# Cosformer attention into a squared-ReLU layer on one core: features of batch 1's queries and keys apart, and a new order of all operations

## The chip, the core and the metric

The kernel runs on one core of one Trainium2 chip. The core has a matrix engine (TensorE, PE in the profile; its weight loads are PEld), a vector engine (VectorE, DVE), an activation engine (ScalarE, ACT), GpSimd (POOL) and SyncE (SP). Each runs its own instructions in order and waits for the others through semaphores. POOL, SP and ACT also issue DMAs. The metric is the device time of one execution in microseconds (us), the median of several runs; before the change it is 275.71 us (275.62 to 275.82, 3 runs).

## What is computed

Attention with cosine and sine features, without a softmax, and then two matrix products with a squared ReLU between them. There are 8 batches of 576 rows, 8 heads of 64 columns; the second part works on 4608 tokens of 512 columns, with 2048 hidden ones.

```python
def phi(x, c, s):
    r = np.maximum(x, 0.0)
    return np.concatenate([r * c, r * s], axis=-1)
q_p = phi(q, cos_w, sin_w)
k_p = phi(k, cos_w, sin_w)
kv = np.einsum('bhsf,bhsd->bhfd', k_p, v)
z = np.sum(k_p, axis=2)
num = np.einsum('bhsf,bhfd->bhsd', q_p, kv)
den = np.einsum('bhsf,bhf->bhs', q_p, z)[..., None] + 1e-06
x = (num / den)            # then heads side by side: 4608 x 512
h = x @ w_in               # 512 -> 2048
out = np.maximum(h, 0) ** 2 @ w_out
```

## The kernel before

**Batches and stages.** Each batch of 576 rows is cut into four blocks of 128 rows (j = 0 to 3) and a tail of 64 rows (t). For each batch b the kernel loads keys and queries into one float32 tile kq (1 MB each) with their tails in kqt, and the values in three parts into vs and vst (`ldkB`, `ldqB`, `ldktB.g`, `ldqtB.g`, `ldvB.i`). It makes the features in bfloat16: `cosB.j` and `sinB.j` (the functions `cos_part`, `sin_part`, L451 on DVE, L449 on ACT) write the tile fe, their tails the tile fet. `vsB.i` spreads the values into vext (L433). `kvB` multiplies key features with values on PE (40 matmuls, tile kz), `kvzB` copies the result out. The query features are turned on PE (`qTB.j`, copied by `qTcB.j`) for batches 0 and 1 and by a transposing DMA on SP (`qTdB.i`) for the others. `numB.j` is the numerator and denominator on PE, `divB.j` the division on DVE (three instructions, L599 to L605) into xp, and xp is turned again (`xTB.j` and `xTcB.j`, or the DMA `xTdB.i`) into xT.

The second part takes xT. For batch 0 and part of 1 and 2 it is a plain product `HB.s.tokhalf` (four or eight matmuls, tile hps), then its ReLU (`...r`) and square (`...q`). For the rest it is a two-by-two product with seven instead of eight blocks: `GB.s.P1` to `P7` with sums `xsB.n` of xT and `w1sn` of the weights, and with evacuations `seed`, `u2`, `s5`, `c11r`, `c12r`, `c21r`, `c22r`. The last product is `Y0.a0` to `a15` and `b0` to `b15` for batch 0 (tile yh, plain; `a` for the first half of the tokens, `b` for the second), and `YB.P1` to `P7` with sums `YB.Sn` and `w2tn` for the others; `YB.stI` stores.

**What sets the order.** The prologue is written out by hand. All the rest is a set of operations in a planner (class Plan), with an engine, a list of predecessors and the tiles that each uses; the string ORDER gives the sequence in which they are emitted, and with it the order on every engine. A star behind a name puts an operation on ACT that could also go to DVE. The planner's own estimates pick the slots of the tiles. Loads that are issued ahead of the planned part are entered with `plan.given(name, time)`: the time at which the order assumes that they have landed. These are the four quarters each of w_in and w_out (`w1_in`, `w2_in`), the query tail of batch 0 (`qt0`), and q, k, their tails and v of batch 1.

**The queue of early loads.** POOL issues, in order, the first loads of batch 0, the four quarters of w_in, the query tails of batch 0 and the first quarter of w_out. Behind the last of the four query features of batch 0 (`cos0.2`, `cos0.3`, `sin0.2`, `sin0.3`, the list `first`), `loads_of_1` issues on POOL q, its tails, k, its tails, the second quarter of w_out, v of batch 1, and the last two quarters of w_out. Loads of batch 2 are on POOL too, at the places that ORDER gives them: `ldv2.0` stands in it ahead of the last of these features. Loads from batch 3 on are on SP, beside the transposing DMAs and the stores. kq has one slot, so a load of the next batch waits until the features of the last one are made; vs has one slot also.

**Products that wait for early loads.** `H0.s.tokhalf` needs a quarter of w_in each. `Y0.a0` to `a3` and `Y0.b0` to `b3` need the first quarter of w_out and a square of H0, `a4` and `b4` on need the second, `a8` and `b8` the third, `a12` and `b12` the fourth. `qT1.j` needs query features, `kv1` all key features and the spread values.

Of the kernel before, what the change touches and what calls it, by code (L numbers as in the profile page):

```python
# [25 lines left out]
num0.3 div0.3 xT0.2 H0.3.00.0 xT0.3 H0.2.00.0 xTc0.2 xTc0.3* H0.1.10.0 H0.1.10r H0.2.10.0
H0.2.00r* H0.0.01.0 H0.0.01r* H0.1.01.0 H0.1.01r* H0.0.10.0 H0.2.10r* H0.1.11.0 f0.t1 H0.0.00r
H0.1.00r H0.1.00q H0.3.00r Y0.a0 f0.t0* qT0.4 H0.0.10r H0.1.10q H0.0.11.0 H0.0.11r* w1s1 Y0.a1
Y0.a2 H0.2.11.0 qTc0.4* H0.2.11r* w1s2 w1s4 Y0.a3 H0.2.01.0 cos1.3 H0.1.11r* H0.2.01r* H0.3.10.0
H0.3.10r* H0.3.10q sin1.0* Y0.b0 Y0.b1 Y0.b2 Y0.b3 H0.3.01.0 H0.3.00q sin1.3* sin1.t cos1.t  # L30
H0.3.11.0 H0.3.11r cos1.1 Y0.b4 H0.3.01r* Y0.b5 Y0.b6 Y0.a4 Y0.a5 cos1.2* sin1.1* qT1.4 qTc1.4*
vs1.1* sin1.2 qT1.3 ldqt2.1 Y0.a6 Y0.a7 cos1.0 qT1.0 vs1.0 qTc1.3* vs1.2 kv1 H0.3.11q* qT1.1
H0.1.01q Y0.a8 Y0.a9 Y0.b7 qTc1.1 kvz1* num1.1 ldq2 qTc1.0 qT1.2 H0.1.11q* Y0.b8 Y0.b9 Y0.b10
div1.1 xT1.1 qTc1.2* num1.2 ldk2 H0.3.01q* ldkt2.1 w2t1 Y0.b11 Y0.b12 Y0.b13 Y0.b14 div1.2 xT1.2
w2t2 xTc1.1* num1.0 ldqt2.0 div1.0 Y0.b15 xTc1.2* Y0.c10* w2t3 Y0.a10 vs2.0* Y0.a11 Y0.a12
ldkt2.0 xT1.0 xTc1.0* num1.3 div1.3 Y0.a13 ldqt3.0 Y0.a14 Y0.c11* Y0.a15 Y0.c00 ldqt3.1
H1.2.00.0 H1.2.00r ldv2.2 xT1.3 ldv2.1 sin2.1 H1.0.01.0 Y0.c01* Y0.st0 xTc1.3* H1.1.11.0 cos2.1
cos2.0* H1.3.10.0 H1.0.01r* ldkt3.0 H1.1.01.0 H1.3.10r* cos2.2* sin2.0 cos2.3 sin2.2 sin2.3
H1.3.00.0 H1.3.00r* vs2.2* H1.0.00.0 sin2.t* H1.1.11r* H1.2.10.0 cos2.t Y0.st1 vs2.1 ldkt3.1
H1.0.10.0 H1.0.10r qTd2.0 qTd2.1 ldv3.0 w2t4 H1.2.10r* H1.3.10q H1.2.01.0 H1.1.01r* H1.1.01q*  # L40
kv2 kvz2* ldv3.2 H1.1.10.0 H1.1.10r* H1.1.10q* H1.2.01r* ldk3 num2.1 div2.1 H1.1.00.0 H1.1.00r*
H1.0.11.0 H1.3.00q num2.2 H1.2.11.0 H1.3.11.0 H1.0.11r* ldq3 H1.2.11r* H1.0.00r H1.1.00q* div2.2
num2.3 H1.1.11q H1.3.11r* H1.3.01.0 H1.3.01r* H1.3.01q* Y1.P10 div2.3 num2.0 Y1.seed Y1.P11
Y1.seed1 ldqt4.1 H1.3.11q vs3.2 Y1.P20 vs3.0* Y1.P21 Y1.c111* Y1.S1 Y1.S2 Y1.P6 xTd2.1 div2.0
Y1.S3 Y1.c110 Y1.u2* cos3.0* sin3.1 cos3.1 cos3.2* sin3.0 sin3.2 sin3.3* num1.4 div1.4 cos3.3*
Y1.P5 ldv4.2 Y1.S4 ldv3.1 vs3.1 H2.1.10.0 xTd2.0 xs2.1 H2.1.10r* qTd2.2 H2.0.11.0 H2.0.11r*
sin3.t* Y1.P7 qTd3.0 xT1.4 xTc1.4 Y1.s5 Y1.c22 xs2.2 H2.0.00.0 G2.2.P1 qTd3.1 H2.1.00.0 xs2.4
ldv4.0 H2.0.01.0 cos3.t* kv3 H2.1.00r* H2.0.00r* G2.2.seed H2.1.11.0 kvz3* xs2.3 H2.0.01r
H2.1.00q num3.0 div3.0 vs4.2* ldk4 H2.1.11r* H2.1.11q G2.2.P2 G2.2.c11r* ldq4 H2.1.01.0 ldkt4.0
w1s3 G2.2.P6 qTd3.2 num3.1 ldqt4.0 H2.1.01r* H2.1.01q* vs4.0* div3.1 G2.2.u2* H2.0.10.0 H2.0.10r  # L50
Y1.P3 Y1.c12 ldv4.1 num3.2 H2.1.10q* div3.2 ldv5.2 G2.2.P5 G2.3.P1 G2.2.s5* G2.3.seed G2.2.P7
G2.2.c22r G2.3.P5 num3.3 xTd3.0 G2.3.s5* div3.3 xTd3.1 G2.3.P2 G2.3.c11r* G2.3.c11q G2.3.P6
Y1.st0 G2.3.u2* G2.2.P4 G2.2.c21r* sin4.3* G2.2.P3 G2.2.c12r ldkt4.1 cos4.1 G2.3.P3 ldkt5.0
# [30 lines left out]
G5.3.seed G5.2.P6 G5.1.c22q* sin7.3 G5.2.P3 G5.2.u2 G5.2.c12r G5.2.P2 xTd6.0 G5.2.c11r* G5.3.P6
G5.3.P2 G5.2.P7 G5.2.c22r G5.3.c11r qTd6.2 G5.3.u2* vs7.1* G5.3.P5 G5.3.s5* G5.1.c11q G5.3.P7
cos7.3* Y4.P4 Y4.c21* xTd6.1 G6.0.P1 G5.3.c22r G5.3.P4 cos7.t* G5.3.c21r* G6.0.seed sin7.t
G5.3.P3 cos7.2 G5.2.P4 kv7 G5.3.c11q xs6.1 G6.0.P5 xs6.2 G6.0.P6 G6.1.P1 G5.3.c12r qTd7.0
G5.3.c22q xs6.3 G6.0.u2 kvz7* num7.0 div7.0 Y4.st1 G6.0.s5* G5.2.c21r* Y5.P1 G5.1.c21q* Y5.seed
G5.3.c21q G6.0.P3 num7.1 G6.0.c12r G6.0.P2 G6.1.seed qTd7.2 Y4.st0 G5.3.c12q Y5.S1 qTd7.1 Y5.P2
# [1493 lines left out]
```

## Time and profile before

| what | value |
|---|---|
| median of 3 runs | 275.71 us |
| the profiled execution, whole | 275.77 us |
| its span, first to last instruction | 273.5 us |
| mean granted TensorE clock | 0.996 |
| ACT busy | 191.0 us, 70% |
| moved by DMA | 53.0 MB, 194 GB/s over the span |
| PE's last matmul ends | 268.8 us |

The page and the timelines give every instruction of each engine with its start from the span's start, its duration, and in square brackets how long the engine stood idle before it and what ended that time. A group of equal instructions in a row is one line with its count (x8). DMA issues are instructions of the engine that issues them; the time to landing is listed apart. The chain of waits goes back from the last instruction, at each step to what released it. Line numbers are those of the kernel before.

The mean share of the sixteen DMA engines is 0.99 to 1.16 in the stretches up to 160 us (it can pass 1 as packets of several queues overlap) and 0.15 from 200 us on.

### The profile page before, as it was taken

How to read it: one execution, taken by the hardware profiler on the slowest of the kernel's cores; microseconds unless marked ns; L12 is line 12 of the kernel's file. 1: busy time of each engine (PE TensorE's matmuls, PEld its weight loads, DVE VectorE, ACT ScalarE, POOL GpSimd, SP SyncE). 2: the span in 40 equal slices, each digit the busy share in tenths (PEclk: the TensorE clock that was granted, in tenths of full speed). 3: DMA queues.
4: the chain of work that ended last, by engine and by line, in shares of the span. 5: the costliest groups of instructions: out<-in, count | busy, mean ns of one | idle time of the engine just before them, and what ended most of it. 6: DMA issues, size and time to landing. Idle time of an engine off the chain costs nothing.

```text
span 273.5 us, 6782 instructions
## 1 busy us (share of the span) xinstructions
PE 264.0 (97%) x2787; PEld 224.0 (82%) x2792; DVE 223.8 (82%) x399; ACT 191.0 (70%) x298; POOL 29.0 (11%) x47
## 2 busy tenths in 40 slices
PE   8999989999999999999999999999999999999993
PEld 3578657689889888999888998799988888888882
DVE  3775887978998999999899998999847948888941
ACT  5754489699688997898799866984669447656300
POOL 8934536100000000000000000000000000000000
PEclk9999999999999999999999999999999999999998
DMA  6999999799999999999996999757142000110116
GB/s 220 318 205 273 343 292 296 225 296 242 293 164 286 301 248 252 354 209 292 210 362 119 232 264 301 159 175 101 36 116 98 0 2 1 76 80 2 77 35 198
DMA packets 79006, 53.00 MB, mean 194 GB/s; under 512 B 52064, under 2 KB 74592, under 8 KB 78976
## 3 DMA queue, kind: packets, MB, share of 16 engines
q1 hardware_dynamic: 71344, 38.28, 57.4%
q0 software_dynamic: 7040, 13.76, 19.0%
q10 hardware_dynamic: 592, 0.52, 0.6%
q8 instruction: 22, 0.36, 0.5%
q14 instruction: 8, 0.07, 0.1%
HBM read 36.70 MB, written 9.44 MB: 169 GB/s over the span
## 4 chain that ended last, share of the span: by engine, by line
PE 75%; DMA 14%; POOL 4%; DVE 2%; ACT 1%; issue 1%; SPq 0%; DVEq 0%; POOLq 0%; ACTq 0%
PE ya L462 17%; PE yb L462 14%; PE hb L462 12%; PE hc L462 8%; PE ha L462 8%; DMA w1sb<-in_moe_w_in_dram 5%; PE hps L462 4%; PE yh L462 4%; DMA kq<-in_q_dram 3%; DMA kqt<-in_k_dram 3%; PE kz L462 3%; DMA xT<-xp 3%; PE num L462 3%; PE yc L462 2%; POOL kq L503 1%; POOL w1sb L412 1%
## 5 line engine op out<-in xcount | busy, mean ns | idle before, releaser
L462 PEld LDWEIGHTS <-w1sb 128*128 128x128 bf16 x736 | 70.5, 98 | 9.6 <-issue 0.9
L462 PEld LDWEIGHTS <-gs 128*128 128x128 bf16 x512 | 49.5, 98 | 6.6 <-DVE gs L459 0.8
L462 PEld LDWEIGHTS <-gT 128*128 128x128 bf16 x448 | 43.1, 98 | 11.7 <-issue 1.5
L462 PE MATMUL hps<-xT,w1sb 128*128 128x256 bf16 x320 | 38.2, 273 | 0.5 <-DMA xT<-xp 0.4
L443 ACT ACTIVATE gT<-gT 128x1024 bf16<-128x1024 bf16 x35 | 36.7, 1061 | 2.1 <-DVE gT L456 1.7
L449 ACT ACTIVATE fe<-kq,cols 128x1024 bf16<-128x1024 f32 (+1 forms) x34 | 33.7, 1032 | 3.5 <-DMA kq<-in_k_dram 2.9
L462 PEld LDWEIGHTS <-w1s 128*128 128x128 bf16 x312 | 29.8, 98 | 3.8 <-issue 0.4
L451 DVE TENSOR_SCALAR fe<-kq,cols 128x1024 bf16<-128x1024 f32 (+1 forms) x38 | 25.4, 705 | 6.7 <-DMA kq<-in_k_dram 5.6
L462 PE MATMUL ya<-w2sb,gT 128*128 128x256 bf16 x256 | 30.7, 273 | 0.1
L462 PE MATMUL hb<-xs,w1sb 128*128 128x256 bf16 x208 | 30.1, 272 | 0.1
L462 PE MATMUL ha<-xT,w1sb 128*128 128x256 bf16 x176 | 26.2, 272 | 0.0
L445 DVE TENSOR_TENSOR gT<-gT 128x1024 bf16<-128x1024 bf16 x37 | 24.9, 685 | 0.2
L605 DVE TENSOR_TENSOR xp<-num,den 128x512 bf16<-128x512 f32 (+1 forms) x33 | 22.2, 675 | 1.1
L456 DVE CUSTOM_DVE_ANT_0 gT<-hb,s 128x512 bf16<-128x512 f32 x26 | 17.8, 686 | 4.8 <-PE hb L462 4.5
L437 ACT ACTIVATE gT<-hps 128x512 bf16<-128x512 f32 x29 | 16.3, 592 | 7.7 <-PE hps L462 7.0
L433 ACT COPY hb<-ha 128x512 f32<-128x512 f32 x26 | 15.2, 586 | 8.7 <-PE ha L462 3.7
L459 DVE TENSOR_TENSOR gs<-gT 128x2048 bf16<-128x2048 bf16 x16 | 19.5, 1220 | 1.2 <-ACT gT L443 0.9
L456 DVE CUSTOM_DVE_ANT_0 gT<-hc,u 128x512 bf16<-128x512 f32 x26 | 17.7, 685 | 2.6 <-PE hc L462 2.4
L433 ACT COPY u<-hb 128x512 f32<-128x512 f32 x21 | 12.3, 586 | 6.5 <-PE hb L462 6.4
L462 PE MATMUL yh<-w2sb,gT 128*128 128x512 bf16 x60 | 14.9, 379 | 1.7 <-DVE fet L451 1.1
L437 ACT ACTIVATE gT<-hb 128x512 bf16<-128x512 f32 x23 | 13.5, 596 | 4.1 <-PE hb L462 3.2
L462 PE MATMUL hc<-xs,w1s 128*128 128x256 bf16 x104 | 15.6, 272 | 0.3 <-DVE gT L456 0.3
(113 smaller groups left out, 415.1 us busy)
## 6 DMA issues: line engine op xcount, KB each, us to landing
...
```

The lines of the kernel that those rows point to most:

```text
L412: nc.gpsimd.dma_start(out=w1sb[:, :, f0:f1], in_=moe_w_in[:, f0:f1].rearrange("(kb p) f -> p kb f", p=P),)
L433: (nc.scalar.copy if e == "ACT" else nc.vector.tensor_copy)(out=out, in_=in_)
L437: nc.scalar.activation(out=out, in_=in_, func=ACTF.Relu)
L443: nc.scalar.activation(out=out, in_=in_, func=ACTF.Square)
L445: nc.vector.tensor_tensor(out=out, in0=in_, in1=in_, op=ALU.mult)
L449: nc.scalar.activation(out=out, in_=in_, func=ACTF.Relu, scale=col)
L451: nc.vector.tensor_scalar(out=out, in0=in_, scalar1=0.0, scalar2=col, op0=ALU.max, op1=ALU.mult)
L456: nc.vector._custom_dve(dve_ops.TENSOR_ADD_SAT, out=out, in0=in0, in1=in1, s0=BIG, s1=0.0)
L459: nc.vector.tensor_tensor(out=out, in0=in0, in1=in1, op=op)
L462: nc.tensor.matmul(out=out, lhsT=lhsT, rhs=rhs, start=start, stop=stop, skip_group_check=True)
L503: eng.dma_start(out=kq[b][:, "kq".index(nm)][:, hs, js], in_=main_of(nm, b)[:, hs, js])
L605: nc.vector.tensor_tensor(out=x, in0=n4[:, :, :, 0:D].rearrange("p b (k l) d -> p b k l d", l=2), in1=r.rearrange("p b (k l) -> p b k l", l=2)
```

## The change

In `plan_att`, the features of batch 1 become operations for the keys alone (`cos1.jk`, `sin1.jk`, needing k) and for the queries alone (`cos1.jq`, `sin1.jq`, needing q): twenty operations of half the width in place of ten. `kv1` then needs those of the keys, `qT1.j` those of the queries of the same block. The other batches keep their operations. The assumed landing times of the first loads are later. ORDER is another sequence of all operations; the sequence is over a thousand words long, and its first lines are shown. On POOL it moves `ldv2.0` from ahead of `loads_of_1` to behind it (behind `qT1.4` in the sequence), and the small loads of batch 2's tails change places with each other. PE has as many instructions as before (5586 with the weight loads), DVE 378 in place of 367 in the listing that joins equal neighbours.

```diff
 ORDER = """
-xT0.k0 sin0.2* cos0.3 xTc0.k0 xT0.k2 ldv2.0 cos0.2* qT0.2 sin0.3* qTc0.2 xT0.k3 xTc0.k2 qT0.3
-xTc0.k3* H0.1.00.0 num0.2 H0.1.00.1 H0.1.00.2 H0.0.00.0 H0.0.00.1 H0.0.00.2 div0.2 qTc0.3*
...
+xT0.k0 cos0.2* sin0.2* sin0.3 xT0.k2 xTc0.k0 cos0.3* qT0.2 xT0.k3 qT0.3 H0.0.00.0 qTc0.2 num0.2
+div0.2 xTc0.k2* H0.0.00.1 xTc0.k3* H0.0.00.2 H0.1.00.0 H0.1.00.1 H0.1.00.2 qTc0.3* num0.3 xT0.2
...
+H0.0.01.0 H0.0.01r* cos1.2q H0.3.10q* cos1.tq sin1.3q H0.2.11.0 H0.2.11r H0.3.01.0 H0.3.01r*
+qT1.4 ldv2.0 Y0.b3 sin1.2q* qT1.0 qTc1.0* cos1.1q cos1.3k qTc1.4* Y0.a0 Y0.a1 Y0.a2 Y0.a3
+cos1.1k* cos1.tk sin1.0k* cos1.0k* qT1.1 cos1.3q qT1.3 cos1.2k Y0.b4 sin1.tk Y0.a4 Y0.a5 vs1.0*
+sin1.1k* qTc1.1 Y0.b5 Y0.b6 Y0.b7 Y0.a6 sin1.2k qT1.2 vs1.1 sin1.3k* H0.1.11q* vs1.2 kv1 Y0.a7
...
@@ def plan_att(b, got, ve, pe):
-        for j in range(J):
-            n = 2 * H * D
-            c = plan.op(
-                f"cos{b}.{j}",
-                both(0.2 + n * 0.00083, 0.135 + n * 0.00052),
-                lambda e, j=j: cos_part(e, b, j),
-                [got["k"], got["q"]],
-                [kq[b], fe[b, j // 2]],
-            )
...
+        sets = [("", ("k", "q", "kt", "qt"), every[0])]
+        if b == 1:
+            sets = [(nm, (nm, nm + "t"), part) for nm, part in (("k", k_), ("q", q_))]
+        for nm, needs, a in sets:
+            main = [got[x] for x in needs if x in "kq"]
+            tail = [o for x in needs if x not in "kq" for o in got[x]]
+            for j in range(J + 1):
+                n = (a.stop - a.start) * (H if j < J else HH) * D
+                for name, emit in (
+                    ("cos", cos_part if j < J else cos_tail),
+                    ("sin", sin_part if j < J else sin_tail),
+                ):
+                    o = plan.op(
+                        f"{name}{b}.{j if j < J else 't'}{nm}",
+                        both(0.2 + n * 0.00083, 0.135 + n * 0.00052),
+                        lambda e, j=j, a=a, emit=emit: emit(e, b, *((j, a) if j < J else (a,))),
+                        main if j < J else tail,
+                        [kq[b], fe[b, j // 2]] if j < J else [kqt[b], fet[b]],
+                    )
+                    if nm != "q":
+                        f.append(o)
+                    if nm != "k":
+                        fq.setdefault(j // 2, []).append(o)
+                        fq.setdefault((j // 2, j), []).append(o)
...
-        w1_in = [plan.given(f"w1.{i}", t) for i, t in enumerate((16.3, 19.4, 21.9, 24.4))]
-        w2_in = [plan.given(f"w2.{i}", t) for i, t in enumerate((26.5, 35.3, 41.2, 44.4))]
-        qt0 = plan.given("qt0", 24.2, [kqt[0]])
+        w1_in = [plan.given(f"w1.{i}", t) for i, t in enumerate((16.5, 19.5, 22.2, 24.6))]
+        w2_in = [plan.given(f"w2.{i}", t) for i, t in enumerate((27.6, 37.2, 42.4, 45.6))]
+        qt0 = plan.given("qt0", 24.6, [kqt[0]])
...
-            ("q", 29.4, kq[1]), ("k", 32.8, kq[1]),
+            ("q", 30.4, kq[1]), ("k", 33.7, kq[1]),
         )}
-        got["qt"] = [plan.given("qt1", 29.8, [kqt[1]])]
-        got["kt"] = [plan.given("kt1", 33.2, [kqt[1]])]
-        land = [plan.given(f"v1.{i}", t, [vs[1, i]]) for i, t in enumerate((36.7, 38.3, 38.8))]
+        got["qt"] = [plan.given("qt1", 30.9, [kqt[1]])]
+        got["kt"] = [plan.given("kt1", 34.2, [kqt[1]])]
+        land = [plan.given(f"v1.{i}", t, [vs[1, i]]) for i, t in enumerate((38.0, 39.4, 39.8))]
```

More of the change, by code (lines that the diff above doesn't have):

```diff
@@ L23 @@
 ORDER = """
-xT0.k0 sin0.2* cos0.3 xTc0.k0 xT0.k2 ldv2.0 cos0.2* qT0.2 sin0.3* qTc0.2 xT0.k3 xTc0.k2 qT0.3
-xTc0.k3* H0.1.00.0 num0.2 H0.1.00.1 H0.1.00.2 H0.0.00.0 H0.0.00.1 H0.0.00.2 div0.2 qTc0.3*
[L26 to L53, printed above, removed]
@@ L84 @@
[L84 to L89, printed above, removed]
@@ new lines @@
+qTc0.4* H0.1.01.0 H0.1.01r w1s1 H0.1.11.0 H0.1.11r* H0.1.00q* H0.2.00r* H0.3.00q* H0.0.11r* w1s2
+Y0.b0 Y0.b1 Y0.b2 sin1.1q H0.3.10.0 H0.3.10r sin1.0q* sin1.tq H0.3.11.0 H0.3.11r cos1.0q
+H0.0.01.0 H0.0.01r* cos1.2q H0.3.10q* cos1.tq sin1.3q H0.2.11.0 H0.2.11r H0.3.01.0 H0.3.01r*
+qT1.4 ldv2.0 Y0.b3 sin1.2q* qT1.0 qTc1.0* cos1.1q cos1.3k qTc1.4* Y0.a0 Y0.a1 Y0.a2 Y0.a3
+cos1.1k* cos1.tk sin1.0k* cos1.0k* qT1.1 cos1.3q qT1.3 cos1.2k Y0.b4 sin1.tk Y0.a4 Y0.a5 vs1.0*
+sin1.1k* qTc1.1 Y0.b5 Y0.b6 Y0.b7 Y0.a6 sin1.2k qT1.2 vs1.1 sin1.3k* H0.1.11q* vs1.2 kv1 Y0.a7
@@ new lines @@
+H0.1.01q H0.3.11q Y0.a8 kvz1* num1.1 div1.1 Y0.a9 Y0.b8 Y0.b9 ldq2 Y0.b10 qTc1.2* num1.2 xT1.1
+div1.2 Y0.b11 Y0.b12 Y0.b13 w1s4 qTc1.3* num1.0 xT1.2 Y0.b14 ldk2 Y0.b15 div1.0 ldkt3.0 w2t1
+ldkt2.1 ldv2.2 Y0.a10 ldqt3.0 H0.3.01q* xTc1.1* Y0.a11 num1.3 Y0.c10* Y0.c11* Y0.st1 xTc1.2*
+Y0.a12 Y0.a13 div1.3 w2t3 xT1.0 Y0.a14 Y0.a15 xT1.3 Y0.c01 cos2.1 vs2.0* xTc1.0* H1.3.00.0
+sin2.0 xTc1.3* H1.1.11.0 H1.3.00r* H1.3.10.0 Y0.c00* ldqt2.0 H1.1.01.0 H1.2.00.0 cos2.0* cos2.2*
+sin2.1 cos2.3 sin2.3 H1.2.01.0 sin2.2* H1.2.00r* H1.3.00q* H1.0.01.0 H1.1.01r vs2.2 H1.2.01r
@@ new lines @@
+ldqt2.1 ldkt2.0 cos2.t ldv2.1 vs2.1* H1.0.01r H1.2.10.0 H1.0.11.0 sin2.t H1.1.10.0 Y0.st0
+H1.2.10r* H1.0.10.0 H1.3.10r H1.1.01q* H1.1.10r* qTd2.0 w2t2 kv2 qTd2.1 w2t4 ldv3.0 H1.3.10q
+H1.1.11r* ldv3.2 kvz2* ldq3 H1.0.11r* H1.0.00.0 num2.1 div2.1 H1.0.10r* H1.1.10q H1.0.00r*
+H1.1.00.0 H1.1.00r* H1.1.11q* H1.3.11.0 H1.3.11r* H1.1.00q num2.2 div2.2 H1.2.11.0 H1.2.11r*
+H1.3.11q H1.3.01.0 H1.3.01r* H1.3.01q* ldk3 num2.3 Y1.P10 Y1.seed Y1.P11 div2.3 Y1.S1 Y1.seed1
+Y1.S2 num2.0 div2.0 Y1.S3 ldqt4.1 ldqt3.1 Y1.P20 ldkt3.1 vs3.0* xTd2.1 vs3.2* Y1.P21 Y1.c111*
@@ new lines @@
+sin3.1 Y1.P6 Y1.u2* cos3.1 cos3.0* sin3.0 num1.4 ldv3.1 Y1.P5 sin3.2 sin3.3 Y1.P7 vs3.1 cos3.3*
+div1.4 H2.1.10.0 cos3.2* Y1.c110* ldv4.2 H2.1.10r* xTd2.0 xs2.3 H2.0.11.0 qTd2.2 Y1.s5* cos3.t*
+H2.0.00.0 H2.0.00r* qTd3.0 qTd3.1 H2.1.00.0 xT1.4 Y1.c22 H2.1.00r* ldv4.0 H2.0.01.0 H2.0.01r*
+H2.0.11r* G2.2.P1 G2.2.seed sin3.t xTc1.4 kv3 kvz3* vs4.2* H2.1.11.0 H2.1.11r* H2.1.00q Y1.S4
+ldq4 xs2.1 xs2.2 xs2.4 num3.0 div3.0 G2.2.P2 G2.2.c11r* H2.1.01.0 H2.1.11q w1s3 ldk4 H2.1.01r*
+H2.1.01q* G2.2.P6 num3.1 div3.1 ldv5.2 G2.2.u2* H2.0.10.0 H2.0.10r ldqt4.0 vs4.0* ldkt5.0
@@ new lines @@
+vs7.1 sin7.t G5.3.c12r xs6.1 xs6.2 xs6.4 xs6.3 cos7.3* qTd7.1 cos7.t* kv7 G6.0.P5 G6.0.seed
+G5.2.c21r* G6.1.P1 G5.3.c21r* G5.3.c21q Y4.c21* G6.0.P6 G6.0.u2 kvz7* G6.0.s5* G5.1.c12q num7.0
+div7.0 G6.0.P2 Y4.st1 G6.1.seed G5.3.c22q G6.1.P2 G6.1.c11r G6.0.c11r* Y5.P1 Y5.seed num7.1
+G6.1.P6 G6.0.P7 G6.1.u2* div7.1 Y4.st0 G6.0.P3 G6.0.c12r Y5.P2 num7.2 xTd7.0 G5.3.c12q* Y5.S1
+G6.1.P5 G6.2.P1 Y5.S2 G6.1.P7 G6.0.c22r G6.1.s5* G6.1.P3 G6.1.c12r Y5.P6 Y5.c11 G6.2.seed
+G6.2.P2 G6.1.c22r G6.1.c22q* G6.0.P4 qTd7.2 Y5.P5 div7.2 Y5.S4 num7.3 G6.0.c21r Y5.s5* G6.1.P4
```

146 lines of the change are left out of this document (63 added, 83 removed).

## The prediction

> **What bounds the kernel now.** I read the page first, then busy time by stage, TensorE's waits, the chain of waits, and the timelines of POOL, TensorE and the SP queue around each wait.
>
> ```profile
> span 273.5 us, 6782 instructions
> PE 264.0 (97%) x2787; PEld 224.0 (82%) x2792; DVE 223.8 (82%) x399; ACT 191.0 (70%) x298; POOL 29.0 (11%) x47
> ```
>
> TensorE (PE) is the bound: it is busy for 97% of the span. The order of its work changes, its amount does not, so the change is worth what it takes from PE's waits or adds to them. The stages (columns: stretch; its length; busy us and count of each engine; clock; DMA share; GB/s):
>
> ```profile
> 15.30:35.00 19.70, 18.93 (x181) 14.99 (x183) 13.32 (x25) 8.77 (x17) 7.77 (x11) 1.00 1.16 277
> 35.00:54.00 19.00, 17.80 (x193) 11.82 (x193) 16.92 (x32) 15.64 (x20) 7.94 (x11) 1.00 0.99 272
> 54.00:85.00 31.00, 30.50 (x355) 26.95 (x353) 27.71 (x51) 25.75 (x40) 0.00 (x0) 1.00 1.09 253
> 85.00:160.00 75.00, 75.00 (x887) 67.17 (x884) 69.99 (x131) 66.13 (x102) 0.00 (x0) 1.00 1.07 257
> 160.00:200.00 40.00, 39.59 (x437) 35.29 (x436) 35.01 (x63) 27.80 (x46) 0.00 (x0) 1.00 0.74 169
> ```
>
> PE's idle time is early: 0.77, 1.20, 0.50, then 0 and 0.41 us. A 256-column matmul starts every 0.109 us (8 take 0.87 in the chain at 87.45) though its record lasts 0.273, so a gap between starts is some 0.16 us longer than the idle shown. By starts, the waits are 0.17 and 0.29 (at 18.85 and 20.48, for the divisions of batch 0), 0.67 (27.49), 1.26 (37.68), 0.57 (81.47) and 0.88 in three places after 130 (132.97, 175.60, 176.46). TensorE's own list of waits:
>
> ```profile
> PE yh L462 <- DVE fet L451: 1.1, 1, 1.1
> PE yh L462 <- DVE gT L445: 0.5, 1, 0.5
> PE hps L462 <- DMA xT<-xp: 0.4, 1, 0.4
> PE hc L462 <- DVE gT L456: 0.3, 1, 0.3
> ```
>
> The first is at 37.68, but yh reads no fet; it reads the second quarter of w2, issued at 27.46 with 10.2 us to landing: 37.64. That load stands behind others on POOL:
>
> ```profile
> 12.62 0.78 POOL L419 DMA_DIRECT2D w2sb<-in_moe_w_out_dram  x1
> 14.32 0.76 POOL L513 DMA_DIRECT2D vs<-in_v_dram  x1 [0.92 <-DMA kq<-in_q_dram]
> 17.20 0.89 POOL L503 DMA_DIRECT2D kq<-in_q_dram  x1 [2.12 <-DVE qpT L433]
> 24.53 0.90 POOL L503 DMA_DIRECT2D kq<-in_k_dram  x1 [1.94 <-DMA w1sb<-in_moe_w_in_dram]
> 27.46 0.76 POOL L419 DMA_DIRECT2D w2sb<-in_moe_w_out_dram  x1 [0.80 <-DMA w2sb<-in_moe_w_out_dram]
> ```
>
> Issue plus time to landing gives the first w2 quarter 27.2, then v of **batch 2** 28.5, q of batch 1 31.7, k 34.8: one queue drains in order and is late by 8 to 14 us. The old table assumed q at 29.4, k at 32.8 and that w2 quarter at 35.3, some 2 us too early. The new one assumes 30.4, 33.7 and 37.2.
>
> **The change, part by part.**
>
> *Load of v for batch 2 (ldv2.0).* It moves on POOL from before batch 1's loads to behind them. Everything it stood ahead of should land earlier by its own share of the queue, 28.5 − 27.2 = 1.3 us: q at 30.4, k 33.5, w2's second quarter 36.3, v of batch 1 at 37.9, 39.1 and 39.5, the third w2 quarter 42.1 (before 43.4), the fourth 45.4. Bounds: 0 (other traffic takes the room) to 1.3; I take 1.3, because the queue was never empty there. What it now stands before, q and k of batch 2, had the same bytes ahead before.
>
> *First yh product.* I count PE's work in order from the first transpose at 15.32 (0.109 per 256 columns, 0.216 per 512, 0.056 per 128, 0.029 per 65). The old Y0.a0 stands after 10.98 us of work, the new first one, Y0.b0, after 12.08: with the two waits that stay (0.46) and 0.1 for qT0.4 behind the tail features it is reached at 28.0. Its weights land at 27.2; its square H0.1.10q follows the two tail features on DVE (24.73 + 0.7 + 0.3 + 0.6 = 26.4). **−0.67**.
>
> *Split features of batch 1.* Ten operations become twenty: DVE 4 × 0.66 + 2 × 0.40 = 3.4 us become 9 × 0.40 + 4 × 0.28 = 4.7, ACT 4 × 1.07 = 4.3 become 7 × 0.65 = 4.6 (steps from back-to-back rows of L451 and L449; 0.28 is an estimate from the others). The query halves need only q. DVE: after w1s2 (30.4), sin1.1q, H0.3.10r, sin1.tq, H0.3.11r, cos1.0q, cos1.2q, cos1.tq give 33.5, when PE reaches qT1.4 (15.32 + 17.73 + 0.56 = 33.6). Y0.b4 is reached at 37.4 and its w2 quarter landed at 36.3: **−1.26**. kv1 is reached at 40.85; the last key feature leaves ACT at 40.65, vs1.1 leaves DVE at 39.8: +0 to +0.5, I take **+0.2**, and **+0.1** for qT0.4 above. If the 1.3 us do not come, this cover is gone: kv1 waits 1.1, Y0.b4 0.3 and Y0.a8 (reached at 42.6) 0.9.
>
> *w1s4 and w2t1 moved between the divisions of batch 1.* Each is 1.22 us on DVE ahead of div1.0 and div1.3; num1.3 and xT1.3 stand behind those: +0 to +0.4, I take **+0.3**.
>
> *Batch 2 and its turn.* PE now comes 1.3 us sooner to a stage that hung on a chain of DMAs:
>
> ```profile
> 64.04 0.49 SPq L503
> 64.58 9.45 DMA kq<-in_q_dram
> ...
> 74.20 7.23 DMA xT<-xp
> 81.42 0.04 issue
> 81.47 1.03 PE hps L462 x8
> ```
>
> What is late next is xT of batch 2. In the old order six of its features run on DVE from 54.59, 0.66 each, to 58.6, behind the last division of batch 1. In the new one five go to DVE and three to ACT; k of batch 2 lands at 52.9 in both, ACT comes to them at 53.8 after Y0.c00 and ends at 53.8 + 3 × 1.07 = 57.0. SP then comes to its two transposes, ldv3.0, the two of ldv3.2, ldq3 and ldk3 in the same order, some 2 us earlier; vs3.0 and vs3.2 leave ACT at 70.5 and 71.3 and free ldv3.1 and ldv4.2, and xTd2.0 is issued at about 72.7. It took 7.2 us; its twin took 5.7 (69.57 to 75.26). H2.0.00.0 is reached at 78.9, xT lands at 78.4 to 79.9: a wait of 0 to 1.0, I take 0.5 in place of 0.57, **−0.07**.
>
> A page of the Trainium skill speaks against this: "SBUF — State Buffer", section "SBUF: two separate sides", says that a DVE instruction in a two-port mode keeps GpSimd from writing descriptors until it ends, which starves loads issued on POOL. The rows show little: two w2 issues beside six DVE features at 35.11 took 1.62 us, 0.81 each, against 0.76 and 0.78 elsewhere. By the rule the extra DVE features would eat the 1.3 us, and the time would be that of rival 2.
>
> *The rest of the order.* kv3 to kv7 stand at the same PE work in both orders, and so do most numerators. 0.88 us of small waits remain late; a new order has its own. I take **0** net, bounds −0.9 (none) to +2.2 (rival 1).
>
> **Sum:** −0.67 − 1.26 + 0.1 + 0.2 + 0.3 − 0.07 = −1.4 us. The profiled run took 275.77 (span 273.5 and 2.3 around it), 0.06 over the median of 275.71. 275.71 − 1.4 = **274.3**. The final 4.7 us after PE's end keep their stores on the same two queues: 0.
>
> **Rivals.** Differences within 0.2% (0.55 us) count as none.
>
> 1. *Slower: DVE becomes the bound in batches 6 and 7.* From kv7 to the first product of block 8 (46 us of PE work in both), DVE had 53 operations, 37.3 us by row steps; now 58, 41.4, while ACT falls from 26.8 to 23.3. At 160 to 180 DVE was busy for 18.4 of 20 us and PE lost 0.74 there. If each of the two 20 us stretches from 160 to 200 and the two behind them, into which ACT's share moves, loses as much, that is 4 × 0.74 = 3.0 in place of 0.88: 275.71 − 1.4 + 2.1 = 276.4. It decides when DVE's idle time there falls under about 0.5 us in 20. Against it: the longest runs of DVE work between two PE marks are overfull by no more than 0.2 us in the new order.
> 2. *The loads land no earlier.* Then kv1, Y0.b4 and Y0.a8 lose 1.3 between them (a wait at one is cover for the next) in place of 1.93 for the two old waits: −1.93 + 1.3 + 0.3 − 0.07 = −0.4: 275.3. For: the landings are also set by SP's traffic; against: the queue was backlogged throughout.
> 3. *The gain is taken back at batch 2.* If xT still lands at 81.42, H2.0.00.0 starts when it did, with 0.2 us more PE work behind it than before: 275.9. For: 64 to 81 was all DMA in the chain. Against: SP's first steps hang on features that end earlier.
> 4. *More is won.* The waits at 81.47 and half of the late ones go too: −1.4 − 0.5 − 0.45: 273.3 or less.
>
> **Numbers.** Forecast 0.52 (its own range 273.6 to 275.1), rival 1 0.14, rival 2 0.14, rival 3 0.08, rival 4 0.12. Faster by over 0.2%: 0.52 + 0.12 and a third of rival 2, 0.69. Slower: most of rival 1 and a little of 3, 0.14. The same: 0.17. The range leaves out the upper half of rival 1 and the lowest of 4: 272.9 to 276.4.
>
> **What would show it.** Right: q of batch 1 lands near 30.4, k near 33.5; no PE wait over 0.3 us at Y0.b0 and Y0.b4; kv1's first matmul near 41 (41.98 before); H2.0.00.0 near 79.4 (81.47); kv3 near 82.9 (84.68); late waits under 1.5. Wrong: q still at 31.7, a wait of 1 us at kv1, a wait over 1.5 us for xT near 79, or idle PE between 160 and 200 behind gT L456.

## The result, and the profile after

| | before | changed |
|---|---|---|
| median of 9 runs, side by side | 275.53 us (274.82 to 277.21) | 274.31 us (272.54 to 274.61) |
| the profiled execution, whole | 275.77 us | 274.27 us |
| its span | 273.5 us | 272.1 us |
| DVE, ACT busy | 223.8, 191.0 us | 229.0, 185.2 us |
| last matmul ends | 268.8 us | 268.3 us |

The ratio is 0.9938, with a 95% interval of 0.991 to 0.9967: faster by 0.6%. (The ratios, here and below, are estimated from all undisturbed runs of both kernels, and need not equal the quotient of the two medians.) The forecast of 274.3 us held. But the profile shows that two terms which the sum had put at 0 were neither of them 0, and that they nearly cancelled.

The head of the page of the changed kernel. TensorE's work is the same, DVE's grew by 5 us and ACT's shrank by 6, as twenty half features took the place of ten and the star moved between the engines:

```profile
span 272.1 us, 6777 instructions
PE 264.2 (97%) x2787; PEld 224.2 (82%) x2792; DVE 229.0 (84%) x417; ACT 185.2 (68%) x290; POOL 29.0 (11%) x47
```

The stages of the changed kernel (stretch; length; busy us and count of PE, PEld, DVE, ACT, POOL; clock; DMA share; GB/s):

```profile
15.30:35.00 19.70, 19.25 (x194) 16.01 (x195) 14.62 (x31) 12.48 (x22) 8.70 (x13) 1.00 1.17 268
35.00:54.00 19.00, 18.89 (x194) 12.16 (x195) 14.87 (x31) 15.54 (x25) 7.69 (x11) 1.00 1.06 311
54.00:85.00 31.00, 30.69 (x376) 27.20 (x374) 28.06 (x51) 26.12 (x41) 0.00 (x0) 1.00 1.06 245
85.00:160.00 75.00, 73.57 (x849) 65.52 (x847) 68.29 (x130) 64.96 (x100) 0.00 (x0) 1.00 1.07 253
160.00:200.00 40.00, 40.00 (x444) 35.90 (x443) 38.88 (x71) 25.97 (x43) 0.00 (x0) 1.00 0.63 172
```

PE's idle time per stage was 0.77, 1.20, 0.50, 0 and 0.41 us. It is now 0.45, 0.11, 0.31, 1.43 and 0. The early waits are gone; the fourth stage, which had none, has the largest.

The early part went as worked out. POOL's issues in the changed kernel (the load of v for batch 2 is now the last of these rows, behind the last quarters of w_out):

```profile
16.94 0.90 POOL L504 DMA_DIRECT2D kq<-in_q_dram  x1 [3.43 <-ACT xT L434]
26.41 0.78 POOL L420 DMA_DIRECT2D w2sb<-in_moe_w_out_dram  x1
...
34.15 1.52 POOL L420 DMA_DIRECT2D w2sb<-in_moe_w_out_dram  x2 [1.17 <-DMA kq<-in_k_dram]
35.64 0.84 POOL L514 DMA_DIRECT2D vs<-in_v_dram  x1
```

With its time to landing, the load of q landed at 30.67 (31.68 before), k at 33.87 (34.83), the second w_out quarter at 37.05 (37.64), the third at 42.58 (43.44). In this execution the quarters of w_in landed some 0.7 us later than in the profile of before, though the change doesn't touch them (the last section shows how far they spread), so the move itself gave more than these differences. Y0.b0 and Y0.b4 have no wait: by starts, nothing over 0.23 us stands between 22 and 79 us.

What is new is at 100 us. PE's waits, then PE's and DVE's rows there, in the changed kernel:

```profile
PE ha L463 <- DMA xT<-xp: 0.9, 1, 0.9
PE yb L463 <- DVE gs L460: 0.4, 1, 0.4
PE hps L463 <- DMA xT<-xp: 0.3, 1, 0.3
```

```profile
100.14 0.61 PE L463 MATMUL ha<-xT,w1sb 128*128 128x256 bf16 x4 [0.90 <-DMA xT<-xp]
...
105.52 1.70 PE L463 MATMUL yb<-w2t,gs 128*128 128x256 bf16 x14 [0.41 <-DVE gs L460]
```

```profile
101.10 0.42 DVE L460 TENSOR_TENSOR xs<-xT 128x512 bf16<-128x512 bf16 x1 [1.91 <-DMA xT<-xp]
101.44 0.69 DVE L434 CAST vext<-vs 128x1024 bf16<-128x1024 f32 x1
102.05 0.68 DVE L446 TENSOR_TENSOR gT<-gT 128x1024 bf16<-128x1024 bf16 x1
102.65 0.42 DVE L460 TENSOR_TENSOR xs<-xT,xs 128x512 bf16<-128x512 bf16 x1
102.98 1.22 DVE L460 TENSOR_TENSOR gs<-gT 128x2048 bf16<-128x2048 bf16 x1
104.24 1.23 DVE L460 TENSOR_TENSOR gs<-gs,gT 128x2048 bf16<-128x2048 bf16 x1
```

PE needs xT of batch 3 (`xTd3.0`) at 99.1; it was issued 1.2 us sooner than before (92.83 for 94.00) and landed later (100.09 for 99.85). SP's rows, before and after:

```profile
91.50 0.54 SPq L513 DMA_DIRECT2D vs<-in_v_dram  x1
92.09 1.82 SPq L516 DMA_DIRECT2D vst<-in_v_dram  x2
94.00 3.19 SPq L650 DMA_TRANSPOSE xT<-xp  x2
```

```profile
92.19 0.53 SPq L514 DMA_DIRECT2D vs<-in_v_dram  x1
92.83 3.70 SPq L652 DMA_TRANSPOSE xT<-xp  x2
```

The load of vs is `ldv4.1`, 0.5 MB. It stands ahead of `xTd3.0` in both orders: 2.50 us ahead before, with the two small loads of `ldv5.2` between, and now 0.64 us, with nothing between. From issue to landing `xTd3.0` took 5.84 us before and 7.26 now. By starts PE waited 1.06 us for it. The second wait, 0.57, follows from the twin: `xTd3.1` landed at 100.98, DVE stood 1.91 us at `xs3.1` for it, and behind it in DVE's order stand `vs4.1`, a square, a second sum of xT, and then the sums `Y2.S1` and `Y2.S2` that `Y2.P6` reads.

How far PE lags is seen by a start less the PE work ahead of it (the prices of the prediction); where the lag grows, PE lost time. PE's end is here the start of its last matmul and 0.109 us, so that 4.84 us are left where the prediction has 4.7:

| lag at | kv1 | kv2 | kv3 | kv4 | kv5 | kv6 | kv7 | PE's end | from there to the span's end |
|---|---|---|---|---|---|---|---|---|---|
| before | 17.78 | 17.87 | 18.97 | 19.17 | 19.28 | 19.61 | 20.46 | 20.68 | 4.84 |
| changed | 16.47 | 16.56 | 17.32 | 19.10 | 19.72 | 19.84 | 19.97 | 20.19 | 3.91 |

So 1.65 us were won up to kv3, nearly all of it was lost again by kv4, 0.42 came back behind it (the 0.74 at 175 is gone, two of 0.22 and 0.23 near 122 us stand against it), and PE ended 0.49 us sooner. The 0.42 may be chance: the first kernel below has the old order at 175 us too, and no wait there. The other 0.93 of the span's 1.42 us came behind PE's last matmul, where nothing had been expected. SP's stores there, before and after:

```profile
267.96 3.09 SPq L1070 DMA_DIRECT2D out_dram<-y  x3
```

```profile
267.26 2.04 SPq L1062 DMA_DIRECT2D out_dram<-y  x3
```

Three issues take 2.04 us, or 3.09 where the third waits. Before, the third was issued at 270.56. It uses the same semaphore as a store that ACT issued at 265.16 and that landed at 270.50. In the new order the stores of `Y8.c12` go out at 262.14, ahead of those of `Y8.c22` at 263.83; the store with that semaphore landed at 267.92, and the last one on SP left at 268.80.

### The profile page after: what moved, and what is told of

Same layout as the page of the kernel before. It is cut to its first block, busy times and chain, and to the rows that moved or that the text cites. A ratio compares the mean times of both kernels' runs of the same rounds, so it can differ in the third digit from the quotient of the medians.

```text
span 272.1 us, 6777 instructions
## 1 busy us (share of the span) xinstructions
PE 264.2 (97%) x2787; PEld 224.2 (82%) x2792; DVE 229.0 (84%) x417; ACT 185.2 (68%) x290; POOL 29.0 (11%) x47
## 4 chain that ended last, share of the span: by engine, by line
PE 58%; DMA 25%; DVE 8%; POOL 4%; issue 2%; ACT 1%; SPq 1%; DVEq 0%; POOLq 0%; ACTq 0%
PE ya L463 14%; PE yb L463 12%; PE hb L463 10%; DMA kq<-in_q_dram 8%; DMA kq<-in_k_dram 8%; PE hc L463 7%; PE ha L463 7%; DMA xT<-xp 4%; DMA vs<-in_v_dram 3%; DMA kqt<-in_q_dram 2%; PE hps L463 2%; PE yc L463 2%; PE kz L463 2%; DVE fe L452 2%; PE num L463 2%
## 5 line engine op out<-in xcount | busy, mean ns | idle before, releaser
L444 ACT ACTIVATE gT<-gT 128x1024 bf16<-128x1024 bf16 x33 | 34.7, 1055 | 10.5 <-DVE gT L457 6.5
L463 PE MATMUL hps<-xT,w1sb 128*128 128x256 bf16 x320 | 37.6, 273 | 0.3 <-DMA xT<-xp 0.3
L450 ACT ACTIVATE fe<-kq,cols 128x1024 bf16<-128x1024 f32 (+1 forms) x35 | 31.9, 953 | 3.4 <-DMA kq<-in_k_dram 1.8
L452 DVE TENSOR_SCALAR fe<-kq,cols 128x1024 bf16<-128x1024 f32 (+1 forms) x45 | 28.3, 666 | 5.7 <-DMA kq<-in_k_dram 5.1
L446 DVE TENSOR_TENSOR gT<-gT 128x1024 bf16<-128x1024 bf16 x39 | 26.4, 685 | 0.7 <-ACT gT L438 0.4
L438 ACT ACTIVATE gT<-ha 128x512 bf16<-128x512 f32 x21 | 12.6, 600 | 8.9 <-PE ha L463 8.8
L463 PE MATMUL yb<-w2t,gs 128*128 128x256 bf16 x128 | 15.3, 273 | 0.4 <-DVE gs L460 0.4
L463 PE MATMUL hb<-xs,w1s 128*128 128x256 bf16 x104 | 15.6, 272 | 0.1
```

What stands on the lines that cost most here:

```text
L438: nc.scalar.activation(out=out, in_=in_, func=ACTF.Relu)
L444: nc.scalar.activation(out=out, in_=in_, func=ACTF.Square)
L446: nc.vector.tensor_tensor(out=out, in0=in_, in1=in_, op=ALU.mult)
L450: nc.scalar.activation(out=out, in_=in_, func=ACTF.Relu, scale=col)
L452: nc.vector.tensor_scalar(out=out, in0=in_, scalar1=0.0, scalar2=col, op0=ALU.max, op1=ALU.mult)
L463: nc.tensor.matmul(out=out, lhsT=lhsT, rhs=rhs, start=start, stop=stop, skip_group_check=True)
```

## The experiments

Each is compared with the kernel before in runs on the same chip, and each has one profile, of one execution. Most are moves of a few names in ORDER; lines not shown only shift their breaks.

**The end alone** (kernel before, with `Y8.c12` and its stores ahead of `Y8.P7`, and the sum `Y8.S3` behind `Y8.P5`).

```diff
-Y8.S2 G8.3.c21q Y8.S4 Y8.seed1 Y7.c22 Y8.P5 Y8.s5* Y8.P6 Y8.u2* Y8.P3 Y8.S3 Y8.P7 Y8.c22
-Y8.st111 Y8.st101 Y8.c12 Y8.st001 Y8.st011 Y7.P4 Y7.c21 Y7.st1 Y8.P4 Y8.c21* Y8.st110 Y8.st100
+Y8.S2 G8.3.c21q Y8.S4 Y8.seed1 Y7.c22 Y8.P5 Y8.S3 Y8.s5* Y8.P6 Y8.u2* Y8.P3 Y8.c12 Y8.st001
+Y8.st011 Y8.P7 Y8.c22 Y8.st111 Y8.st101 Y7.P4 Y7.c21 Y7.st1 Y8.P4 Y8.c21* Y8.st110 Y8.st100
```

> The kernel before with four moves in its last stretch only: the copy Y8.c12 and its two stores stand ahead of Y8.c22 and its stores, and the sum Y8.S3 behind Y8.P5, as in the changed kernel. Theory A (the end counts: the stores of block 8 are issued 1 to 2 us sooner, so that the last store on SP doesn't wait for an earlier store's landing): from PE's last matmul to the end of the span 3.9 us in place of 4.8, time 0.9 us under the kernel before, PE's waits unchanged. Theory B (the shorter end of the changed kernel was chance): 4.8 us as before, time within 0.3 us.

Measured: 274.63 us against 275.69, ratio 0.9977 (0.9949 to 1.0004). From PE's end to the span's end 3.89 us (4.84 before), with this row of SP's stores:

```profile
267.86 2.08 SPq L1070 DMA_DIRECT2D out_dram<-y  x3
```

The third store no longer waits, so the mechanism of the end is shown by the profile. That the whole time falls by as much is not: the interval reaches past 1.

**The load alone** (kernel before, with only `ldv2.0` behind `loads_of_1`).

```diff
-xT0.k0 sin0.2* cos0.3 xTc0.k0 xT0.k2 ldv2.0 cos0.2* qT0.2 sin0.3* qTc0.2 xT0.k3 xTc0.k2 qT0.3
+xT0.k0 sin0.2* cos0.3 xTc0.k0 xT0.k2 cos0.2* qT0.2 sin0.3* qTc0.2 ldv2.0 xT0.k3 xTc0.k2 qT0.3
```

> The kernel before with one move: ldv2.0 behind the loads of batch 1 on POOL. Theory A (the early gain is taken back where batch 3's transposed x lands): q of batch 1 lands near 30.4, k near 33.5, the second w2 quarter near 36.3; the wait at 37.68 falls from 1.26 to under 0.4 us; kv3 starts 0.7 to 1.2 us sooner than 84.5; behind it a wait for xT of batch 3 near 99 gives back half or more, so that the time is 0 to 0.6 us under the kernel before. Theory B (an early gain stays to the end): time 1.0 to 1.3 us under. Theory C (the landings are set by other traffic): no landing moves by over 0.3 us, time the same.

Measured: 274.09 us against 275.69, ratio 0.9949 (0.9921 to 0.9976). q landed at 30.35, k at 33.52, the second w_out quarter at 36.21, the third at 41.93, and neither 27.49 nor 37.68 has a successor. The second and fourth stage of this kernel:

```profile
35.00:54.00 19.00, 19.00 (x207) 12.97 (x205) 17.22 (x32) 15.61 (x21) 7.47 (x11) 1.00 1.04 302
85.00:160.00 75.00, 75.00 (x872) 67.30 (x871) 70.49 (x131) 65.07 (x100) 0.00 (x0) 1.00 1.08 262
```

PE is never idle in either. The lag is 16.36 at kv1, 17.41 at kv3, 17.54 at kv4 and 18.53 at PE's end: what is won early stays won (the profiled execution, 273.18, is the fastest of its twelve). The theory that any early gain must be given back at batch 3 expected otherwise, and missed. By the ratio the gain is 1.4 us, where the theory that it stays had 1.0 to 1.3. The other two profiles of the old order with this load moved, further down, have no wait between 100 and 106 us either, so the loss there belongs to the new order.

**The load put back** (changed kernel, `ldv2.0` ahead of `loads_of_1` again).

```diff
-xT0.k0 cos0.2* sin0.2* sin0.3 xT0.k2 xTc0.k0 cos0.3* qT0.2 xT0.k3 qT0.3 H0.0.00.0 qTc0.2 num0.2
+xT0.k0 cos0.2* sin0.2* sin0.3 xT0.k2 ldv2.0 xTc0.k0 cos0.3* qT0.2 xT0.k3 qT0.3 H0.0.00.0 qTc0.2
...
-qT1.4 ldv2.0 Y0.b3 sin1.2q* qT1.0 qTc1.0* cos1.1q cos1.3k qTc1.4* Y0.a0 Y0.a1 Y0.a2 Y0.a3
+H0.3.01r* qT1.4 Y0.b3 sin1.2q* qT1.0 qTc1.0* cos1.1q cos1.3k qTc1.4* Y0.a0 Y0.a1 Y0.a2 Y0.a3
```

> The changed kernel with one move undone: ldv2.0 again ahead of the loads of batch 1. Theory A: these land 1.2 to 1.4 us later, PE waits 0.8 to 1.3 us in all at Y0.b4, kv1 and Y0.a8, kv3 starts up to 1.2 us later than 82.9; but the wait for xT of batch 3 at 100.1 shrinks by as much, and the time is 0 to 0.4 us over the changed kernel's. Theory B: the time is 0.9 to 1.3 us over it.

Measured: 275.16 us against 275.69, ratio 0.9981 (0.9952 to 1.0011). q landed at 32.30, k at 35.74. PE's waits in two stretches, joined by a line of dots:

```profile
33.47 1.91 PE L463 MATMUL hps<-xT,w1sb 128*128 128x256 bf16 x16 [1.45 <-DVE gT L440]
35.53 0.40 PE L625 MATMUL tq<-ident,fet 128*128 128x128 bf16 x4 [0.16 <-DVE fet L452]
...
105.91 1.92 PE L463 MATMUL yb<-w2t,gs 128*128 128x256 bf16 x16 [1.02 <-DVE gs L460]
```

The new order puts query features on DVE and ACT ahead of ReLUs that PE waits for, so late queries cost 1.62 us by starts at 33.47. Neither theory had a wait there; Y0.b4, kv1 and Y0.a8 have none. In return the wait at 100 us is gone, though the one at 105 grew from 0.57 to 1.19 us, and PE's end lags by 20.12, as in the changed kernel's profile (20.19): there the early loss stands in place of the later one, as theory A has it. The times lean to theory B: 0.9981 here against 0.9938 and (below) 0.9945 for the whole change, with intervals that overlap. The run decides neither.

**xT of batch 3 ahead of `ldv4.1`** (changed kernel, `ldv4.1` moved behind `xTd3.1` on SP).

```diff
-G2.3.u2* G2.2.c21r* sin4.3* ldv4.1 G2.3.P3 cos4.1 G2.3.P7 sin4.1* G2.3.c22r xTd3.0 sin4.0
-cos4.2* cos4.0 cos4.3 Y2.P1 G2.3.P4 G2.3.c21r* num3.4 sin4.2 xTd3.1 G2.3.c12r Y2.seed xs3.1
+G2.3.u2* G2.2.c21r* sin4.3* G2.3.P3 cos4.1 G2.3.P7 sin4.1* G2.3.c22r xTd3.0 sin4.0 cos4.2*
+cos4.0 cos4.3 Y2.P1 G2.3.P4 G2.3.c21r* num3.4 sin4.2 xTd3.1 ldv4.1 G2.3.c12r Y2.seed xs3.1 Y1.P4
```

> The changed kernel with one move: ldv4.1 (0.5 MB of values) behind both transposing DMAs xTd3.0 and xTd3.1 on SP instead of ahead of them. Theory A (1.6 us are lost at 100.1 and 105.5 because xT of batch 3 stands behind a load): xT lands 1.5 us sooner, both waits fall under 0.3 us, kv4 starts near 105.6 in place of 107.3, and the time is 272.5 to 273.0. Theory B (the transposes are late for what was queued long before, q and k of batch 4): they land within 0.5 us of where they did and the time is within 0.4 us of the changed kernel's. Theory C (vs4.1, later now, holds up kv4): a new wait of over 0.5 us at kv4.

Measured: 273.05 us against 275.69, ratio 0.9917 (0.9882 to 0.9951). The transposes landed at 98.32 and 99.39, and the wait at 100 us is gone. The second one stayed. DVE's and PE's rows of this kernel:

```profile
101.56 0.69 DVE L434 CAST vext<-vs 128x1024 bf16<-128x1024 f32 x1 [1.17 <-DMA vs<-in_v_dram]
```

```profile
105.64 1.59 PE L463 MATMUL yb<-w2t,gs 128*128 128x256 bf16 x13 [0.72 <-DVE gs L460]
```

The load that was moved back now lands at 101.54, and DVE stands for it at `vs4.1`, with the same sums behind: the wait, 0.88 us by starts, went to the next thing in DVE's order. That the profile's own span is only 0.4 us shorter has to do with its start: its first transpose on PE came at 16.80 (15.45 in the changed kernel). The interval of the ratio overlaps that of the whole change, so a gain over the changed kernel is not shown by this run's times.

**The same, and `vs4.1` behind the sums** (the version before, with `vs4.1` behind `Y2.S1` and `Y2.S2` on DVE).

```diff
-G2.3.c21q* G2.3.c12q* ldkt4.1 vs4.1 Y1.st0 G3.0.P1 G3.0.seed Y1.c21* ldkt4.0 Y2.P2 G3.0.P2
-G3.0.c11r* qTd4.0 G3.0.P5 G2.3.c22q G3.1.P1 G3.1.P5 xs3.2 qTd4.1 Y2.S1 Y2.S2 ldv5.0 ldq5 ldk5
+G2.3.c21q* G2.3.c12q* ldkt4.1 Y1.st0 G3.0.P1 G3.0.seed Y1.c21* ldkt4.0 Y2.P2 G3.0.P2 G3.0.c11r*
+qTd4.0 G3.0.P5 G2.3.c22q G3.1.P1 G3.1.P5 xs3.2 qTd4.1 Y2.S1 Y2.S2 vs4.1 ldv5.0 ldq5 ldk5
```

> The changed kernel with ldv4.1 behind both transposing DMAs of batch 3 and, in addition, vs4.1 on DVE behind the sums Y2.S1 and Y2.S2. Theory A (the wait of 0.9 to 1.2 us at 105.6 comes from DVE standing at vs4.1 for its load while the sums for Y2.P6 queue behind it): this wait falls under 0.2 us, kv4 starts 1.6 to 1.8 us sooner against its PE work than in the changed kernel, time 0.6 to 1.0 us under that of the run with ldv4.1 alone, some 272.2 to 272.5. Theory B (the sums are late for their inputs gT): the wait stays over 0.6 us.

Measured: **272.24 us** against 275.58, ratio 0.9873 (0.9837 to 0.9909), the fastest of all. Neither wait is left at 100 to 106 us; the lag is 17.65 at kv4 (19.10 in the changed kernel) and 19.02 at PE's end (20.19). One wait is new, 0.55 us by starts:

```profile
118.44 0.60 PE L463 MATMUL hb<-xs,w1sb 128*128 128x256 bf16 x4 [0.39 <-ACT u L434]
```

Whether it comes in each execution was not tried. Two names moved give 0.9873 in place of 0.9938, and the intervals just don't meet: what the change lost at batch 3 was lost by the order on SP and DVE there, not by any engine's amount of work. `xTd3.0` took 5.35 and 5.01 us to landing in the two kernels with `ldv4.1` behind it, and 7.26, 6.31 and 6.13 in the three profiles of the new order with `ldv4.1` just ahead (the changed kernel, the load put back, the changed kernel once more).

**Load and end together in the old order** (the kernel before with both moves shown above, its features whole).

> The kernel before with the two moves that worked, together: ldv2.0 behind the loads of batch 1, and the last block's copy and stores in the changed kernel's order. Theory A (the changed kernel's gain is these two, and the rest of its order and the split features add nothing): PE's end 18.4 to 18.8 us over its work as with the first move alone, the end 3.9 us, time 273.0 to 273.8 on a chip where the kernel before takes 275.7, so at or below the changed kernel. Theory B (the split and the new order carry part of the gain): 0.5 us or more above the changed kernel.

Measured: 273.60 us against 275.58, ratio 0.9935 (0.9907 to 0.9963). Lag 17.57 at kv3, 19.30 at PE's end (18.4 to 18.8 expected), 3.92 us from there; this execution has 0.44 us of wait for the third w_out quarter at 42.64, and the two waits at 174 and 175 us (0.33 and 0.42) of the profile before. Two moves in the old order give as much as the whole change, 0.9938: as the new order stands, nothing measurable is left for the split and for its other thousand places together. (With its loss at batch 3 undone it gave 0.9873, above.)

**The split alone** (the kernel before with `ldv2.0` moved, and the ten features cut in halves that stand side by side on the same engine; the old assumed landing times).

```diff
-Y0.a2 H0.2.11.0 qTc0.4* H0.2.11r* w1s2 w1s4 Y0.a3 H0.2.01.0 cos1.3 H0.1.11r* H0.2.01r* H0.3.10.0
+Y0.a2 H0.2.11.0 qTc0.4* H0.2.11r* w1s2 w1s4 Y0.a3 H0.2.01.0 cos1.3q cos1.3k H0.1.11r* H0.2.01r*
-H0.3.10r* H0.3.10q sin1.0* Y0.b0 Y0.b1 Y0.b2 Y0.b3 H0.3.01.0 H0.3.00q sin1.3* sin1.t cos1.t
+H0.3.10r* H0.3.10q sin1.0q* sin1.0k* Y0.b0 Y0.b1 Y0.b2 Y0.b3 H0.3.01.0 H0.3.00q
+sin1.3q* sin1.3k* sin1.tq sin1.tk cos1.tq cos1.tk H0.3.11.0 H0.3.11r cos1.1q cos1.1k Y0.b4
```

The other features are halved in the same way, and `plan_att` is that of the changed kernel.

> The kernel before with ldv2.0 moved and the split features, the halves side by side where the whole operation stood, query half first. Theory A (the split by itself only costs: 6 times 0.14 us on DVE, 4 times 0.23 on ACT): kv1 0 to 0.6 us later against its PE work than with ldv2.0 moved alone, time 0 to 0.5 us over that. Theory B (query halves first let the turns of q start sooner): kv1 or the turns sooner, time 0.3 us or more under that.

Measured: 274.61 us against 275.58, ratio 0.9949 (0.992 to 0.9977), the ratio of the load alone (0.9949). The split by itself adds nothing that can be measured. The profile, of the slowest of the twelve executions, can't settle where kv1 comes: its second w_in quarter landed at 20.58, the latest of all profiles, and PE lost 1.06 us by starts to it.

**The new order without the split** (changed kernel; each feature of batch 1 whole, at the place of its query half).

```diff
-        if b == 1:
+        if b < 0:
...
-Y0.b0 Y0.b1 Y0.b2 sin1.1q H0.3.10.0 H0.3.10r sin1.0q* sin1.tq H0.3.11.0 H0.3.11r cos1.0q
+Y0.b0 Y0.b1 Y0.b2 sin1.1 H0.3.10.0 H0.3.10r sin1.0* sin1.t H0.3.11.0 H0.3.11r cos1.0 H0.0.01.0
```

> The changed kernel without the split: each feature of batch 1 is one operation for k and q again, standing where its query half stood. Theory A (the split is needed by this order: the features stand early, and k lands 3.2 us after q): DVE idles some 3 us before 34, PE waits 2 us or more between 30 and 42, kv1 near 43.5 in place of 41.4, and a time of 1 to 2.5 us over the changed kernel's, less what the waits at 100 and 105 give back. Theory B (the split gives nothing here either): kv1 within 0.4 us.

Measured: 278.64 us against 275.58, ratio 1.0105 (1.006 to 1.015), more than expected, and kv1 at 49.53 where 43.5 was expected (the profiled execution, 280.33, is the slowest of the six). PE's two large waits, and then windows about them (columns as in the stages above):

```profile
36.92 1.03 PE L462 MATMUL hps<-xT,w1sb 128*128 128x256 bf16 x8 [2.53 <-DVE gT L439]
39.95 0.60 PE L624 MATMUL tq<-ident,fet 128*128 128x128 bf16 x4 [2.00 <-DVE fet L451]
```

```profile
34.00:38.00 4.00, 1.43 (x12) 0.88 (x10) 2.49 (x4) 2.49 (x4) 2.80 (x4) 1.00 1.11 326
38.00:42.00 4.00, 1.83 (x13) 1.50 (x15) 4.00 (x8) 1.62 (x3) 0.08 (x1) 0.50 1.16 204
42.00:46.00 4.00, 4.00 (x26) 2.04 (x24) 0.59 (x2) 3.40 (x4) 2.42 (x3) 0.64 1.09 258
...
37.00:38.00 1.00, 0.95 (x8) 0.60 (x7) 1.00 (x2) 1.00 (x3) 1.00 (x2) 1.00 0.98 322
38.05:39.00 0.95, 0.00 (x0) 0.00 (x0) 0.95 (x3) 0.95 (x3) 0.03 (x1) 0.50 1.06 205
```

Whole features wait for k too (DVE stood until 35.51 for it), and the ReLUs that PE needs stand behind them. What the expectation lacked is in the third column from the right, the clock: it fell to 0.50 at 38.0 us, as the second wait began, and stayed there until 44.8. The mean clock of this kernel's six runs is 0.985 to 0.994, and 0.996 or more in every run of the other kernels with a change, so it seems to have fallen in each of the six. A smaller part is this execution's own: 0.90 us of wait by starts at 29.44 for the first w_out quarter, which landed at 29.31 (27.75 in the changed kernel). So the new order needs the split, with these features where their query halves stand, though the split alone is worth nothing.

**The changed kernel once more**, unaltered, to see how much of the wait at 100 us is chance.

> The changed kernel again, unaltered, since its nine times fell into two groups, 272.5 to 273.0 and 274.3 to 274.6. Theory A (the two groups are with and without the waits at 100.1 and 105.5, 1.6 us together): the times are again in two groups some 1.6 us apart, and the profile shows both waits if its time is in the upper group and neither if it is in the lower. Theory B (the start decides: the first loads land at other times in each execution): the times spread without a gap, and the waits at 100 to 106 are over 1 us whatever the time.

Measured: 274.35 us (12 runs, 272.53 to 275.27 without a gap) against 275.38, ratio 0.9945 (0.9918 to 0.9973). PE's waits in this execution:

```profile
43.85 0.59 PE L463 MATMUL yh<-w2sb,gT 128*128 128x512 bf16 x2 [0.98 <-DMA w2sb<-in_moe_w_out_dram]
...
104.71 1.92 PE L463 MATMUL yb<-w2t,gs 128*128 128x256 bf16 x16 [0.34 <-DVE gs L460]
```

Here xT of batch 3 landed at 98.41, in time, and only 0.51 us by starts is left of the second wait. A wait for the third w_out quarter at 43.85 (1.14 by starts), which the first profile does not have, stands in its place. The span is 270.8 us. So the loss of 1.6 us at batch 3 is one draw: it was 0.5 in the second. Of theory A the small loss in a fast execution came, and not the two groups of times; of theory B the spread without a gap came, and not the wait of over 1 us whatever the time.

## Why the prediction was right, point by point

- *The number* came out right in part by luck: two terms put at 0 were +1.2 and −0.9 us in the profile (the two points marked failed).
- *What bounds the kernel* held up to PE's last matmul: PE is busy for 97%, and every gain or loss until there is one of its waits. The 0.93 us behind it are not.
- *The load of v.* Right in cause: alone it gives 0.9949, where the whole change gives 0.9938. Up to 1.3 us sooner was forecast for all that it stood ahead of: q in the old order landed at 30.35 (30.4 forecast), k at 33.52 (33.5), the second w_out quarter at 36.21 (36.3), the third at 41.93 (42.1). In the changed kernel's profile they came at 30.67, 33.87, 37.05 and 42.58, behind quarters of w_in that were some 0.7 us late. The rule of the Trainium skill's page "SBUF — State Buffer" (section "SBUF: two separate sides") that was held against this left no mark: the two issues at 34.15, beside DVE features with one ReLU between them, took 1.52 us, 0.76 each. (The prediction misread DVE's rows for the two issues at 35.11 in the kernel before: from 34.92 to 37.67 there were three features and two squares, not six features.)
- *Y0.b0, −0.67, and Y0.b4, −1.26*: both waits are gone. *qT0.4 and kv1, +0.1 and +0.2*: the lag at kv1 fell by 1.31. Early loads that the change doesn't touch landed late in this execution and cost PE 0.46 us: 0.31 by starts at 16.09, for a query feature of batch 0 on ACT, whose load landed at 14.68 (14.03 before), and 0.15 at 17.31 for the first w_in quarter (17.26, before 16.57). Without them the lag fell by 1.77, where −0.67 − 1.26 + 0.3 = −1.63 was forecast. kv1's first matmul came at 41.40 (41 forecast).
- *num1.3 and xT1.3, +0.3*: mis-sized. The lag grows by 0.09 us from kv1 to kv2, as it did before, so nothing came there.
- *xT of batch 2, a wait of 0.5*: 0.47 at 79.58 (79.4 forecast); kv3 came at 82.87 (82.9). The 84.68 that the prediction gives for kv3 before is from the chain of waits; its first matmul started at 84.52, so it came 1.65 us sooner, where 1.8 was forecast.
- *The rest of the order, 0*: failed as a sum of one execution. 1.63 us of new waits at 100 and 105 us, and 0.42 won back later. The prediction followed the transposing DMA of batch 2 through its queue and did not do so for batch 3, where the same pattern (PE earlier, the landing not) returned, with the 0.5 MB load that stood 2.50 us ahead of it now 0.64 us ahead. Late waits under 1.5 us were forecast; from 85 us on they are 1.06 + 0.57 + 0.45 = 2.1.
- *The final 4.7 us, 0*: failed. It fell by 0.93. "The same two queues" was true and not enough: the order of the stores decides which semaphore the last one has to wait for. This term hid the one above: −1.31 at kv1, −0.34 up to kv3, +1.58 to kv4, −0.42 to PE's end, −0.93 behind it make the −1.42 of the spans.
- *Rival 1, DVE the bound in batches 6 and 7*: fell. DVE is idle for 0.41 us from 160 to 180 us and for 0.71 from 180 to 200, so once under the 0.5 at which it was to decide, and PE lost nothing (busy for 40.00 of 40 us). *Rival 2, loads no earlier*: fell. *Rival 3, given back at batch 2*: not at batch 2, but its mechanism came one batch later. *Rival 4*, 273.3 or less, was not reached by the change. The two further moves went past it, to 272.24, by other waits than those that it names.

What stays open: whether the shorter end shows in the time (alone 0.9977, with an interval past 1), why the first loads land over 1 us apart from one execution to the next, how large the loss at batch 3 is on the mean (1.6 and 0.5 were seen), and how far the load's place matters to the new order (0.9981 without it, 0.9938 with it, intervals overlapping).
